# Linear attention on one core: half of one head's output stored by GpSimd's DMAs

## The chip, the cores and the metric

The kernel runs on one core of a Trainium2 chip. The metric is the time of one execution in device microseconds; the median of the three runs of the kernel before is 168.19 us (167.89 to 168.42). The core's engines are named as in the profile: PE (matrix multiplication; PEld is its weight load), DVE (vector), ACT (activation), POOL (GpSimd) and SP (which here only issues DMAs). Data moves between memory (HBM) and the core's own memory (SBUF) by 16 DMA engines that all issuers share.

## The reference

The input holds 32 heads of 2048 rows by 128 columns, in bfloat16. Each head is linear attention with the feature map elu + 1:

```
phi_q = where(q > 0, q + 1, exp(q)) + 1e-6
phi_k = where(k > 0, k + 1, exp(k)) + 1e-6
kv  = einsum("bhsd,bhse->bhde", phi_k, v)
z   = einsum("bhsd->bhd", phi_k)
num = einsum("bhqd,bhde->bhqe", phi_q, kv)
den = einsum("bhqd,bhd->bhq", phi_q, z)[..., None] + 1e-6
out = num / den
```

## The kernel before

**Layout.** A head lies in SBUF as 128 partitions ("rows" below) of 16 consecutive sequence rows, 16 x 128 bfloat16 values, 4 KB a partition and 512 KB a head. Partition p of the output tile is 4 KB of consecutive memory in the output.

**Stages of one head h.** SP loads k, v and q (`ldk`, `ldv`, `ldq`, line 388; for most heads two at once, 1 MB). phi is split in two parts: min(exp(x), 1) plus eps, and max(x, 0). For k, ACT computes the exponential (`ek`, L416), DVE clamps it (`em`, L392), and POOL makes the positive part (`rk`, L399). POOL also copies v beside a column of ones (`v1`, L429), so that one product gives kv and z. PE multiplies both parts into one accumulator (`kv`, L437) and DVE copies it out (`kvs`, L403). PE transposes q (`T`, L455); ACT and DVE make the two parts from it (`eq` L467, `emq` L392, `rqa` L397, `rqb` L398). PE multiplies with kv in two groups of tiles (`n`, L498, L503, L505), DVE takes the reciprocal of the denominator (`a` L522, `r` L525) and multiplies (`f`, L529) into one of 14 output buffers, `o_sb[:, h % 14]`. SP stores it (`st`, L538).

**Order.** Each engine runs a list of keys written out by hand in `ORDER`; `resolve` puts in the waits that the dependencies need and no others. An engine runs its list in order, so an operation that waits holds up all behind it on that engine. SP's list mixes loads and stores: with 14 output buffers the stores may come long after the computation, and many are put off to the end, where there is nothing left to load. `TIE` makes the positive part `rk` of head h wait for the clamp `em` of head h - 1, which places it behind DVE's clamps.

**Stores.** `st_parts(h)` gives the pieces of a head's store as (first tile, last tile, first row, last row). Most heads are one piece of all 128 rows. Head 2 is stored in pieces of 51, 64 and 13 rows, the first half of head 3 in pieces of 68 and 60, and head 31, the last, in three pieces by tiles as they become ready. Head 11, the twelfth, is one store, `st11.0`, placed behind the load of v for heads 28 and 29 and issued at 116.31 us. Its buffer is used again by head 25, whose multiplication `f25` waits for all stores of head 11.

**The end.** After its last store SP waits for each output buffer's semaphore in turn (L556), the last head's at the end.

POOL's list around the change is `... v121.0 v122.0 rk22.0 rk23.0 v123.0 rk24.0 v124.0 ...`. In the key `v122.0` the head is 22 and the last digit its piece: `v1` is the operation.

Of the kernel before, what the change touches and what calls it, by code (L numbers as in the profile page):

```python
# [14 lines left out]
NO, NE, NR, NV, NQ, NK = 14, 2, 2, 2, 4, 2  # L15
# [45 lines left out]
def groups(h):  # L61
    if h == NH - 1:
        return ((0, 2, 3, 0), (6, 2, 3, 2), (12, 2, 2, 4))
    return ((0, 4, 3, 0), (12, 2, 2, 4))
# [3 lines left out]
ROWS = {2: ((0, 51), (51, 115), (115, 128))}  # L68


def st_parts(h):
    tiles = ((0, 6), (6, 12), (12, 16)) if h == NH - 1 else WHOLE
    if h in HALF:
        tiles = HALVES
    return tuple((a, b, x, y) for i, (a, b) in enumerate(tiles)
                 for x, y in (HALF.get(h, ()) if i == 0 and h in HALF else ROWS.get(h, ((0, P),))))
# [5 lines left out]
def eps_dve(h, i):  # L82
    return i == 1 or h in EPD


def on(key, eng):
    return ON.get(key, eng)
# [11 lines left out]
def rqb_parts(h):  # L99
# [4 lines left out]
    if h == NH - 1:  # L104
# [48 lines left out]
    "POOL": """  # L153
        ident0 ident v10.0 v13.0 rk5.0 rk4.0 v14.0 v15.0 v16.0 rk6.0 rk7.0 v17.0 rk8.0 v18.0 v19.0 rk9.0
        rk10.0 v110.0 v111.0 rk11.0 v112.0 rk12.0 v113.0 rk13.0 v114.0 rk14.0 v115.0 rk15.0 v116.0 rk16.0
        rk17.0 v117.0 rk18.0 v118.0 v119.0 rk19.0 v120.0 rk20.0 rk21.0 v121.0 v122.0 rk22.0 rk23.0 v123.0
        rk24.0 v124.0 v125.0 rk25.0 v126.0 rk26.0 rk27.0 v127.0 v128.0 rk28.0 rk29.0 v129.0 rk30.0 v130.0
        rk31.0 v131.0
    """,
# [18 lines left out]
def _ap(base: bass.AP, elem_offset: int, dims):  # L178
    return bass.AP(base.tensor, base.offset + elem_offset, [list(base.ap[0])] + [list(d) for d in dims])


class Program:
# [10 lines left out]
    def add(self, eng, key, fn, deps=(), dma=None, inc=True):  # L193
        assert key not in self.op, key
        self.op[key] = (eng, fn, tuple(deps), dma, inc)
# [71 lines left out]
def bass_standalone__linear_attn_elu__prompt_kernel(nc: bass.Bass, q: bass.AP, k: bass.AP, v: bass.AP, out: bass.AP):  # L267
    B, H, S, D = q.shape
    assert D == P and S == 16 * P and B * H == NH
    NT = S // P  # L270
# [5 lines left out]
    qf, kf, vf, of = (t.rearrange("b h s d -> (b h) s d") for t in (q, k, v, out))  # L276
    rows = lambda t, h: t[h].rearrange("(p j) d -> p j d", j=NT)

    with ExitStack() as es:
        names = [0]  # L280

        def alloc(make, shape, dt):
            names[0] += 1
            return es.enter_context(make(f"la_{names[0]}", shape, dt))
# [5 lines left out]
        sb = lambda shape, dt=bf16: alloc(nc.sbuf_tensor, shape, dt)  # L290
# [6 lines left out]
        o_sb = sb([P, NO, NT, D])  # L297
# [7 lines left out]
        pr = Program(sem)  # L305
        add = pr.add
# [3 lines left out]
        def over(name, h, parts, t0, t1):  # L310
            return [f"{name}{h}.{i}" for i, (a, b) in enumerate(parts(h)) if a < t1 and t0 < b]

        def every(name, h, parts):
            return [f"{name}{h}.{i}" for i in range(len(parts(h)))]
# [8 lines left out]
        def used(buf, n, heads, key):  # L323
            for h in heads:
                u = users[buf, h % n]
                assert u[0] == h, (buf, h, u[0])
                u[2].append(key)

        def fs(h, banks):
            return [f"f{h}.{i}" for i, (t0, nb, n, b0) in enumerate(groups(h))  # L330
                    if set(banks) & set(range(b0, b0 + nb))]

        def both(h, p=pair):
            return (h - h % 2, h - h % 2 + 1) if p(h) else (h,)

        def first(h):
            return both(h)[0]

        def spans(h, t0, t1):
            if len(both(h)) == 1:  # L340
                return [(h, t0, t1)]
            at = [(x, *(min(max(t - 8 * (x - first(h)), 0), 8) * 2 for t in (t0, t1))) for x in both(h)]
            return [(x, a, b) for x, a, b in at if a < b]

        def rqs(h, t0=0, t1=NT):
            return [d for x, a, b in spans(h, t0, t1) for d in
                    ([f"rqa{x}"] if a < na(x) else []) + over("rqb", x, rqb_parts, a, b)]
# [57 lines left out]
        def head(h):  # L405
# [71 lines left out]
            if blk == len(two) - 1:  # L477
                for x in two:
                    out_of(x)

        def out_of(h):
            two, h0 = both(h), first(h)
            blk = h - h0

            def tile(buf, t):
                if len(two) == 1:
                    return buf[:, h % NQ, t]
                at = t % 8 * 2
                return buf[:, (h0 + t // 8) % NQ, at:at + 2].rearrange("p u d -> p (u d)").rearrange("p (m x) -> p m x", x=2)[:, :, blk]

            for i, (t0, nb, m, b0) in enumerate(groups(h)):
                late = eps_dve(h, i)

                def g(e, t0=t0, nb=nb, m=m, b0=b0, late=late):
                    for b in range(nb):
                        o = 512 * (b0 + b)
                        if not late:
                            e.matmul(_ap(o_ps[:, :], o + D, [[NC, m]]), lhsT=ones[:], rhs=epsr[:, 0:m], start=True,  # L498
                                     stop=False, skip_group_check=True)
                        for c in range(m):  # L500
                            t = t0 + b * m + c
                            to = o_ps[:, o + NC * c:o + NC * (c + 1)]
                            e.matmul(to, lhsT=tile(emq_sb, t), rhs=kvs_sb[:, h % NK, 0:NC], start=late and c == 0,  # L503
                                     stop=False, skip_group_check=True)
                            ins = e.matmul(to, lhsT=tile(rq_sb, t), rhs=kvs_sb[:, h % NK, 0:NC], start=False, stop=True,  # L505
                                           skip_group_check=True)
                    return ins
                banks = range(b0, b0 + nb)
                t1 = t0 + nb * m
                key = f"n{h}.{i}"  # L510
                add("PE", key, g, [d for x, a, b in spans(h, t0, t1) for d in over("emq", x, q_parts, a, b)] + [f"kvs{h}", "ones", "eps1", "eps2"] + rqs(h, t0, t1)
                    + (fs(h - 1, banks) if h else []) + ([f"kvs{h + 1}"] if 5 in banks and h + 1 < NH else []))
                for buf, n in (("emq", NQ), ("rq", NQ)):
                    used(buf, n, two, key)
                used("kvs", NK, (h,), key)
                den = _ap(o_ps[:, :], 512 * b0 + D, [[512, nb], [NC, m]])
                rden = rden_sb[:, h % 2, t0:t1].rearrange("p (a b) -> p a b", b=m)
                done = [key]
                if 5 in banks and h + 2 < NH and GAP == 3:
                    done += every("kv", h + 2, kv_parts) if on(f"kvs{h + 2}", "DVE") == "DVE" else [f"kvs{h + 2}"]  # L520
                if late:
                    add("DVE", f"a{h}.{i}", lambda e, rden=rden, den=den: e.tensor_scalar(  # L522
                        rden, den, EPS, None, op0=ALU.add), done)
                    done, den = [f"a{h}.{i}"], rden
                add("DVE", f"r{h}.{i}", lambda e, rden=rden, den=den: e.reciprocal(rden, den), done)  # L525

                def g(e, t0=t0, t1=t1, nb=nb, m=m, b0=b0):
                    first = lambda t: t.offset
                    return e.tensor_tensor(  # L529
                        out=_ap(o_sb[:, :, :, :], first(o_sb[:, h % NO, t0, 0:1]) - first(o_sb[:, :, :, :]),  # L530
                                [[m * D, nb], [D, m], [1, D]]),
                        in0=_ap(o_ps[:, :], 512 * b0, [[512, nb], [NC, m], [1, D]]),
                        in1=_ap(rden_sb[:, :, :], first(rden_sb[:, h % 2, t0:t0 + 1]) - first(rden_sb[:, :, :]),
                                [[m, nb], [1, m], [0, D]]), op=ALU.mult)
                add("DVE", f"f{h}.{i}", g, [f"r{h}.{i}"] + fill("o", NO, (h,), f"f{h}.{i}"))
            for i, (a, b, x, y) in enumerate(st_parts(h)):
                key = f"st{h}.{i}"
                add("SP", key, lambda e, a=a, b=b, x=x, y=y: e.dma_start(rows(of, h)[x:y, a:b], o_sb[x:y, h % NO, a:b]),  # L538
                    [f"f{h}.{j}" for j, (t0, nb, m, b0) in enumerate(groups(h)) if t0 < b and a < t0 + nb * m],
                    dma=f"o{h % NO}")  # L540
                used("o", NO, (h,), key)

        for h in range(NH):
            head(h)
# [7 lines left out]
        for e, engine in (("POOL", nc.gpsimd), ("SP", nc.sync), ("ACT", nc.scalar), ("PE", nc.tensor), ("DVE", nc.vector)):  # L552
            pr.emit(e, engine)
        last = f"o{(NH - 1) % NO}"
        for name in [f"o{s}" for s in range(NO) if f"o{s}" in pr.count and f"o{s}" != last] + [last]:
            nc.sync.wait_ge(pr.get(name), pr.count[name])  # L556


# [26 lines left out]
```

## Time and profile before

| what | value |
|---|---|
| median of the runs shown | 168.19 us |
| the profiled execution's own time | 167.83 us |
| its span, first to last instruction | 166.5 us |
| busy: PE, DVE, ACT, POOL | 156.6, 154.6, 146.6, 83.7 us |
| granted TensorE clock, mean | 0.994 |
| bytes read and written in HBM | 50.33 and 16.78 MB, 403 GB/s over the span |
| DMA packets | 16542 |
| head 11's output computed to its store's issue | about 77 to 116.31 us |
| store: issue to landing, median over the kernel | 15.5 us |

Times in the views are microseconds from the start of the span. A line such as `L399 POOL TENSOR_SCALAR` is a group of instructions by source line, engine and operation; the number in brackets behind a line of the timeline is the time the engine was idle before it and the one that ended that idle time. The DMA share is the mean over the 16 DMA engines. It can stand a little above 1, because packets of one engine overlap by a few per cent. The trace also records each arrival of a DMA at its semaphore. A DMA arrives once for each DMA engine that carries a share of it, so the spread of one DMA's 16 arrivals tells how far the 16 engines are apart.

### The profile page before, as it was taken

The page shows a single profiled execution, that of the slowest core. Times are in us where ns is not written, and L with a number is a line of the kernel's source. Part 1 is how long each engine was busy: PE and PEld are TensorE (multiplying, and loading weights), DVE is VectorE, ACT ScalarE, POOL GpSimd, SP SyncE. Part 2 cuts the span into 40 slices and gives each one's busy share as a digit, 9 for nine tenths or more (in the row PEclk, how much of TensorE's full clock was granted, in tenths as well). Part 3 has the DMA queues.
Part 4 walks back from the last instruction along what each step waited for, and adds up shares of the span by engine and source line. Part 5 has one row for each costly group of instructions (what it writes and reads, how often), then busy time and mean ns, then how long its engine had stood idle before and what let it go on. Part 6 is the DMA issues. An engine that isn't in the chain of part 4 may idle for free.

```text
span 166.5 us, 6111 instructions
## 1 busy us (share of the span) xinstructions
PE 156.6 (94%) x2709; PEld 150.9 (91%) x2709; DVE 154.6 (93%) x307; ACT 146.6 (88%) x99; POOL 83.7 (50%) x64
## 2 busy tenths in 40 slices
PE   4999997999999999999999999999999999999950
PEld 1677996999999999999999999999999999999840
DVE  0498999999999999999999999999999999999992
ACT  3799987899999999999999999999999999977700
POOL 1100019655666665555566666655655676634000
PEclk9999999999999999999999999999999999999997
DMA  5999999999999999999999999999999999999997
GB/s 224 410 424 411 422 403 418 403 405 404 420 418 412 414 406 427 411 423 410 417 408 423 415 424 404 420 415 424 407 416 422 413 416 414 416 416 413 385 396 279
DMA packets 16542, 67.51 MB, mean 405 GB/s; under 512 B 1539, under 2 KB 1923, under 8 KB 14723
## 3 DMA queue, kind: packets, MB, share of 16 engines
q1 hardware_dynamic: 16371, 66.59, 98.5%
q8 instruction: 21, 0.34, 0.8%
q10 hardware_dynamic: 144, 0.52, 0.8%
q14 instruction: 6, 0.05, 0.1%
HBM read 50.33 MB, written 16.78 MB: 403 GB/s over the span
## 4 chain that ended last, share of the span: by engine, by line
PE 83%; DMA 7%; DVE 6%; SPq 2%; issue 0%
PE la L437 33%; PE la L503 18%; PE la L505 16%; PE la L455 16%; DMA la<-in_q_dram 7%; DVE la L529 4%; SPq L388 2%; DVE la L398 1%; DVE la L525 1%; PE la L498 0%; DVE la L522 0%; DVE la L403 0%
## 5 line engine op out<-in xcount | busy, mean ns | idle before, releaser
L529 DVE TENSOR_TENSOR la<-la 128x1536 bf16<-128x1536 f32 (+1 forms) x65 | 77.9, 1200 | 0.6
L503 PE MATMUL la<-la 128*128 128x129 bf16 x512 | 66.6, 219 | 0.1
L505 PE MATMUL la<-la 128*128 128x129 bf16 x512 | 66.6, 219 | 0.0
L399 POOL TENSOR_SCALAR la<-la 128x2048 bf16<-128x2048 bf16 x28 | 53.0, 1893 | 26.2 <-DVE la L522 18.7
L467 ACT ACTIVATE la<-la 128x2048 bf16<-128x2048 bf16 (+2 forms) x35 | 60.2, 1728 | 5.0 <-PE la L455 3.1
L416 ACT ACTIVATE la<-la 128x2048 bf16<-128x2048 bf16 (+1 forms) x33 | 61.3, 1865 | 3.4 <-DMA la<-in_k_dram 1.9
L437 PE MATMUL la<-la 128*128 128x129 bf16 x1024 | 63.4, 220 | 0.0
L437 PEld LDWEIGHTS la<-la 128*128 128x128 bf16 x1024 | 59.3, 98 | 0.8 <-DVE la L403 0.4
L429 POOL COPY la<-la 128x1024 int32<-128x1024 int32 (+1 forms) x30 | 31.2, 1043 | 41.1 <-PE la L437 22.7
L505 PEld LDWEIGHTS la<-la 128*128 128x128 bf16 x512 | 49.8, 97 | 0.0
L503 PEld LDWEIGHTS la<-la 128*128 128x128 bf16 x512 | 48.1, 97 | 0.3 <-DVE la L529 0.2
L392 DVE TENSOR_SCALAR la<-la 128x2048 bf16<-128x2048 bf16 (+2 forms) x68 | 42.4, 658 | 1.1 <-ACT la L416 1.1
L455 PE MATMUL la<-la 128*128 128x128 bf16 x512 | 35.3, 222 | 1.0 <-DMA la<-in_q_dram 0.9
L455 PEld LDWEIGHTS la<-la 128*128 128x128 bf16 x512 | 30.7, 99 | 2.7 <-DMA la<-in_q_dram 1.5
L397 ACT ACTIVATE la<-la 128x1024 bf16<-128x1024 bf16 (+2 forms) x29 | 31.6, 1091 | 0.0
L398 DVE TENSOR_SCALAR la<-la 128x1024 bf16<-128x1024 bf16 (+2 forms) x36 | 24.4, 682 | 4.7 <-DMA la<-in_k_dram 4.6
L498 PE MATMUL la<-la 128*128 128x3 bf16 (+1 forms) x128 | 21.6, 168 | 2.5 <-DVE la L529 2.5
L498 PEld LDWEIGHTS la<-la 128*128 128x128 bf16 x128 | 12.5, 98 | 2.8 <-DVE la L529 2.8
L525 DVE RECIPROCAL la<-la 128x12 f32<-128x12 f32 (+1 forms) x65 | 12.9, 200 | 1.0 <-PE la L505 0.2
L403 DVE CAST la<-la 128x129 bf16<-128x129 f32 x32 | 8.3, 258 | 0.0
L368 PE MATMUL la<-la 128*128 128x480 bf16 x21 | 6.7, 468 | 1.5 <-POOL la L353 1.5
L368 PEld LDWEIGHTS la<-la 128*128 128x128 bf16 x21 | 2.3, 120 | 3.9 <-issue 1.7
(15 smaller groups left out, 9.7 us busy)
## 6 DMA issues: line engine op xcount, KB each, us to landing
out_dram<-la SPq DMA_DIRECT2D x29, 512.0 KB, 15.5
la<-in_q_dram SPq DMA_DIRECT2D x14, 1024.0 KB, 17.6
la<-in_v_dram SPq DMA_DIRECT2D x11, 1024.0 KB, 15.0
la<-in_k_dram SPq DMA_DIRECT2D x11, 1024.0 KB, 16.4
la<-in_k_dram SPq DMA_DIRECT2D x10, 512.0 KB, 13.5
la<-in_v_dram SPq DMA_DIRECT2D x9, 512.0 KB, 14.8
la<-in_q_dram SPq DMA_DIRECT2D x4, 512.0 KB, 10.3
la<-in_v_dram ACTq DMA_DIRECT2D x1, 512.0 KB, 5.6
```

What stands on the lines that cost most here:

```text
L392: add(on(key, "DVE"), key, lambda e: e.tensor_scalar(t, t, 1.0, EPS, op0=ALU.min, op1=ALU.add), deps)
L397: "ACT": lambda e: e.activation(dst, src, ACT.Relu),
L399: "POOL": lambda e: e.tensor_scalar(dst, src, BIG, 0.0, op0=ALU.min, op1=ALU.max)}[eng], deps)
L416: add("ACT", key, lambda e, a=a, b=b: e.activation(em_sb[:, h % NE, a:b], k_sb[:, h % NI["k"], a:b], ACT.Exp), [f"ldk{k0}.0"] + fill("em", ...
L429: add(on(key, "POOL"), key, lambda e, a=a, b=b, word=word: e.tensor_copy(v1_sb[:, h % NV, a:b, 0:D].bitcast(word), v_sb[:, h % NI["v"], a: ...
L437: ins = e.matmul(kv_ps, lhsT=src[:, j], rhs=v1_sb[:, h % NV, j, 0:NC], start=(j + part == 0), stop=(j == NT - 1 and part == 1))
L455: ins = e.transpose(to, src, ident[:])
L467: add("ACT", key, lambda e, a=a, b=b: e.activation(part(emq_sb, a, b), src(a, b), ACT.Exp), over("T", h, t_parts, a, b) + fill("emq", NQ, ...
L498: e.matmul(_ap(o_ps[:, :], o + D, [[NC, m]]), lhsT=ones[:], rhs=epsr[:, 0:m], start=True, stop=False, skip_group_check=True)
L503: e.matmul(to, lhsT=tile(emq_sb, t), rhs=kvs_sb[:, h % NK, 0:NC], start=late and c == 0, stop=False, skip_group_check=True)
L505: ins = e.matmul(to, lhsT=tile(rq_sb, t), rhs=kvs_sb[:, h % NK, 0:NC], start=False, stop=True, skip_group_check=True)
L529: return e.tensor_tensor(out=_ap(o_sb[:, :, :, :], first(o_sb[:, h % NO, t0, 0:1]) - first(o_sb[:, :, :, :]), [[m * D, nb], [D, m], [1, D] ...
```

## The change

Head 11's store by SP keeps rows 0 to 63, all 16 tiles. Rows 64 to 127 are stored by four DMAs that POOL issues: rows 64 to 73 (`swx`, 10 rows), 74 to 107 (`swa`, 34 rows), 108 to 110 (`swy`, 3 rows) and 111 to 127 (`swb`, 17 rows). Each of these DMAs names a row as two pieces of 2 KB, the second half first, on both sides, so the same bytes land in the same places. In POOL's list `swx` and `swa` stand behind `rk22.0`, `swy` and `swb` behind `v123.0`. Each waits for both groups of head 11's output, counts on a semaphore of its own, and is waited for by head 25's output and, first of all, at SP's end.

```
+SOFT = 11
+SPREAD = (("swx", 64, 74), ("swa", 74, 108), ("swy", 108, 111), ("swb", 111, 128))
+
+
 def st_parts(h):
+    if h == SOFT:
+        return ((0, 16, 0, 64),)
     tiles = ((0, 6), (6, 12), (12, 16)) if h == NH - 1 else WHOLE
...
     "POOL": """
-        rk17.0 v117.0 rk18.0 v118.0 v119.0 rk19.0 v120.0 rk20.0 rk21.0 v121.0 v122.0 rk22.0 rk23.0 v123.0
+        rk17.0 v117.0 rk18.0 v118.0 v119.0 rk19.0 v120.0 rk20.0 rk21.0 v121.0 v122.0 rk22.0 swx swa rk23.0 v123.0 swy swb
...
+            for key, x, y in SPREAD if h == SOFT else ():
+                half = NT * D // 2
+                sb, dr = o_sb[x:y, h % NO], rows(of, h)[x:y]
+                frm, to = (bass.AP(t.tensor, t.offset + half, [list(t.ap[0]), [-half, 2], [1, half]]) for t in (sb, dr))
+                add("POOL", key, lambda e, to=to, frm=frm: e.dma_start(to, frm),
+                    [f"f{h}.{j}" for j in range(len(groups(h)))], dma=key)
+                used("o", NO, (h,), key)
...
-        for name in [f"o{s}" for s in range(NO) if f"o{s}" in pr.count and f"o{s}" != last] + [last]:
+        for name in [x[0] for x in SPREAD] + [f"o{s}" for s in range(NO) if f"o{s}" in pr.count and f"o{s}" != last] + [last]:
             nc.sync.wait_ge(pr.get(name), pr.count[name])
```

## The prediction

> **What bounds the kernel now.** I read the page first (busy shares, the DMA row of the 40 slices, the queues), then the waits, the busy times in stretches of the tail, the store line L538, GpSimd's timeline around the new operations, and last the semaphore arrivals of each transfer that the trace records (one arrival for each DMA engine that takes part).
>
> The page, its second and third parts:
> ```profile
> DVE  0498999999999999999999999999999999999992
> DMA  5999999999999999999999999999999999999997
> ...
> q1 hardware_dynamic: 16371, 66.59, 98.5%
> ```
> DVE and the 16 DMA engines are both full almost to the end, so both are candidates. The busy times in stretches decide (DMA share is the mean over 16 engines):
> ```profile
> core 0: us, PE busy (x) PEld busy (x) DVE busy (x) ACT busy (x) POOL busy (x), PEclk, DMA share, GB/s
> ...
> 150.00:156.00 6.00, 6.00 (x112) 5.97 (x110) 5.66 (x11) 4.88 (x6) 1.85 (x2) 1.00 1.03 416
> 156.00:158.30 2.30, 1.98 (x34) 1.63 (x31) 2.23 (x8) 0.99 (x1) 0.00 (x0) 1.00 0.88 353
> 158.30:162.00 3.70, 2.09 (x36) 1.92 (x36) 3.60 (x10) 0.00 (x0) 0.00 (x0) 1.00 0.99 396
> 162.00:164.00 2.00, 0.00 (x0) 0.00 (x0) 1.38 (x2) 0.00 (x0) 0.00 (x0) 1.00 0.96 385
> 164.00:166.50 2.50, 0.00 (x0) 0.00 (x0) 0.00 (x0) 0.00 (x0) 0.00 (x0) 0.64 0.57 213
> ```
> After 164 no engine computes; only DMA runs, for 2.5 us, and with 0.57 of its engines. From 156.0 to 158.3 some already run dry (0.88). So the engines do not finish together. The waits of SP's own sequencer, and the store line from 155 on, agree:
> ```profile
> SPq L556 <- DMA out_dram<-la: 2.4, 2, 1.2
> ```
> ```profile
> L538 SPq DMA_DIRECT2D out_dram<-la x6: 332/333/537, 157.4 to 163.4; - x6
> ...
> DMA to landing us min/median/max: 5.3/5.7/6.1
> ```
> The arrivals give the skew. Head 28's store (512 KB, 8 rows of 4 KB per engine) reached its 16 counts at 156.64 us, then 0.07, 0.13, 3.12, 3.14, 3.24, 3.33, 3.91, 4.58, 4.58, 4.64, 4.70, 4.74, 4.75, 4.75 and 4.78 us later. **Three engines lead by 3.1 us, the last trails by 4.8.** From 130 us on every transfer has the 3.1 us step and ends 4.7 to 4.9 us after its first arrival, so the trailing engines never idle. At the end they go back to back: head 30's store ends at 165.18, then head 31's three stores need per engine 8 rows of 1536 B (64.9 ns), 1024 B (45.8) and 1536 B, together 1.40 us, so 166.58 against the 166.48 recorded. Without a backlog the last store could land at 165.23: issued 163.40, plus 1.31 us (head 31's first store, issued 161.63, first arrival 163.46, less 8 x 64.9 ns), plus 0.52. **The end is set by the most loaded DMA engines, 1.25 us after what the compute would allow.**
>
> **What goes.** SP's store of head 11 keeps rows 0 to 63. It gives each engine 8 rows now (128 rows over 16 arrivals); the half kept gives 4. So 4 rows of 4 KB leave every engine: 4 x 161.4 ns (mean packet of that size) = 0.65 us. One SP issue stays, its wait is the same.
>
> **What comes: where the 64 rows land.** The arrivals of before show how rows are shared: SP's store of 51 rows has 3 arrivals from engines, that of 68 has 4, of 60 has 15, of 13 has 13, of 64 or 128 has 16: always the largest number up to 16 that divides the rows. The three engines of the 51-row store took 17 rows each: right after it three stand 2.7 us further back (17 x 161.4 ns = 2.74). By that count 10, 34, 3 and 17 rows make 10, 2, 3 and 1 shares, of 1, 17, 1 and 17 rows: 16 shares in all. I take them to lie side by side on 16 different engines. Then 13 engines get one row (two 2 KB packets of 85.9 ns, 0.17 us), a net 0.65 - 0.17 = 0.47 us less; three get 17 rows, 17 x 0.172 - 0.65 = +2.28 us. If those three are the leaders (lead on the last 4.78), they still end 4.78 - 2.28 - 0.47 = 2.0 us ahead. No row shows where GpSimd's shares go; this is a choice, and the first rival is the other case. What the arrivals do show: if SP always deals from the first engine on, one leader is among the last three engines (it moves 0.12 us ahead just when SP's 13-row store passes three engines by), and none is among the first four (set back by the 51- and the 68-row store).
> The Trainium skill, DMA: Bandwidth & Descriptors, section "Why a DMA increments its semaphore by 16 and not by 1", states the same divisor rule, and that GpSimd's shares go on from a cursor that walks round the engines; started at 0, it would put the 17-row shares on engines 10, 11 and 15. That agrees with what the arrivals show of one leader; no run here shows the cursor.
>
> Small terms: arrivals cost a 4-byte packet of 9.1 ns; if each of the four DMAs posts on every engine, 0.04 us. So -0.47 + 0.04 = **-0.43 us** on the 13 engines. Bounds: -0.48 (3 rows by 161.4, no extras) and 0 (if reading the rows' descriptors costs as much as is saved; nothing in the trace shows that). I take -0.43, since it is the sum of measured packets. It arrives whole at the end, because those engines never idle after 116 us, where head 11 is stored.
>
> **What comes on GpSimd.** Two DMA issues stand after rk22 and two after v123. GpSimd's timeline, with those places (rk22 is the second line, rk23 and v123 the next two):
> ```profile
> 105.99 1.04 POOL L429 COPY la<-la 128x1024 int32<-128x1024 int32 x1 [1.61 <-PE la L437]
> 107.00 1.89 POOL L399 TENSOR_SCALAR la<-la 128x2048 bf16<-128x2048 bf16 x1
> 110.75 1.89 POOL L399 TENSOR_SCALAR la<-la 128x2048 bf16<-128x2048 bf16 x1 [1.85 <-DVE la L522]
> 112.58 1.04 POOL L429 COPY la<-la 128x1024 int32<-128x1024 int32 x1
> 115.37 1.89 POOL L399 TENSOR_SCALAR la<-la 128x2048 bf16<-128x2048 bf16 x1 [1.75 <-DVE la L522]
> ```
> Both places are idle gaps, 1.85 and 1.75 us. They wait only for head 11's output, which is some 40 us old. The trace has no issue by GpSimd. Low end: SP's, 0.33 us (L538). High end: GpSimd's longest usual operation, 1.89 us. I take 1.0, nearest to its copy (1.04), the one that only moves data. Two issues, 2.0 us, overrun each gap by some 0.2 us; at 1.89 by 2.0 us. Behind them queue rk23, v123 and rk24, v124, for which PE waits: rk23 and v123 end at 113.62 and their matmuls (L437) start at 117.81, 4.2 us of cover, and 4.62 us later again. Even the high end is covered on PE's side; SP's loads that wait for these reads are issued over 10 us ahead of landing.
>
> Not covered by that is DVE, which has no idle time here:
> ```profile
> 109.38 1.28 DVE L392 TENSOR_SCALAR la<-la 128x2048 bf16<-128x2048 bf16 x2
> ...
> 114.00 1.29 DVE L392 TENSOR_SCALAR la<-la 128x2048 bf16<-128x2048 bf16 x2
> ```
> GpSimd now idles just while these pairs run. Where the two meet early in a GpSimd operation, GpSimd gives way:
> ```profile
> 144.94 1.53 POOL L429 COPY la<-la 128x1024 int32<-128x1024 int32 x1
> ...
> 144.95 0.63 DVE L392 TENSOR_SCALAR la<-la 128x2048 bf16<-128x2048 bf16 x1
> ```
> The copy went from 1.04 to 1.53 us, DVE's operation stayed at 0.63. So I cost DVE at 0, with a bound of 1.9 us for each gap (a whole GpSimd operation ahead of DVE). A DVE delay d moves the last store's issue and the floor 165.23; the new end is 166.05, so the first 0.8 us cost nothing.
>
> Other edits: SP's four new waits at the end (28 ns each, steps of 0.07 us) fall between 163.74 and 165.2, while SP waits for DMA anyway: 0. Head 25's output overwrites the buffer: head 11's last arrival is now 134.04 against head 25's first multiplication at 135.62 (L529); SP's half comes 0.4 us earlier, and GpSimd's part is issued 20 us before: 0.
>
> **Sum.** The profiled execution took 167.83 us (span 166.5). 167.83 - 0.43 = 167.40. The median of the runs shown, 168.19, lies 0.36 above; so 168.19 - 0.43 = 167.76, forecast **167.75**, own range 167.6 to 168.1.
>
> **Rivals.**
> 1. *The shares fall elsewhere* (slower). Always from the first engine, as SP's do: it would carry 1 + 17 + 1 + 17 = 36 rows, 36 x 0.172 - 0.65 = +5.5 us, 173.7. A 17-row share on an engine that trails: +2.28, 170.5; on one that is 1.5 us ahead of the last: +0.8. It costs as soon as the share's 2.28 us exceed that engine's lead. For it: no row shows GpSimd's order. Against: one leader's place fits. 0.10.
> 2. *All four are dealt over 16 engines* in ceilings (1, 3, 1 and 2 rows each): the first three engines get 7 rows, 7 x 0.172 - 0.65 = +0.56, and they are among the last: 168.75, slower. For it: 128 and 64 rows are dealt so by SP; against: SP's 13, 51 and 60 rows are not. 0.06. The page named above states that GpSimd does deal some plain copies so.
> 3. *Issuing collides with DVE* (slower). If DVE is held up longer than 0.8 us, the floor decides: 1.5 us give 166.73 in the span, 168.4 against the median; 2 us give 168.9. For it: DVE saturated, the gaps coincide with its pairs; against: the overlap at 144.94. 0.16. The Trainium skill, SBUF — State Buffer, section "SBUF: two separate sides", warns that GpSimd cannot write descriptors while certain DVE copies run; by that, issues stall for at most 1.29 us a gap, covered as above, and the time stays the forecast's.
> 4. *Nothing moves*: the gain is spent on fetching descriptors or 2 KB packets under load: 168.0 to 168.4. 0.06.
>
> **Chances.** Forecast 0.62. About 0.3% (0.5 us) is what a measurement here can tell from no change; the forecast's 0.43 lies just inside, with the runs shown spread over 0.5 us, so I split it 0.36 faster, 0.26 within. Rival 3 gives 0.03 within, 0.13 slower; rival 4 0.01 faster, 0.05 within; 1 and 2 0.16 slower. Faster 0.37, within 0.34, slower 0.29. The range runs from 167.4 (0.48 and the runs' spread) to 168.9, which takes in rivals 2 and 4 and most of 3; rival 1 stays out.
>
> **What would show it.** Right: the arrivals' 3.1 us step falls to under 1 us, the 156 to 158.3 stretch has a share near 1.0, the last arrival comes about 0.4 us earlier, packets of 2 KB rise by 128. Wrong: one arrival of late transfers 2 us or more behind all others (rival 1); DVE idle before L392 or longer L392 around 109 to 119 and the last L529 later (rival 3).

## The result, and the profile after

The changed kernel takes **170.12 us** (median of 4 runs, 169.79 to 171.03) against 168.12 for the kernel before on the same chip: ratio 1.0127 [1.0082, 1.0172]. It is slower by 2.0 us, where 167.75 and a range of 167.4 to 168.9 were forecast. The profiled execution is the longest of the four, 171.03 us with a span of 169.7. Lines of kernel.py from 72 on stand lower in the changed file: the store by SP is now L544, SP's waits at the end L569, DVE's clamp L398, GpSimd's positive part L405 and its copy L435; GpSimd's DMAs are issued at L552.

The page of the kernel after, its slices and its queues:
```profile
DVE  0499899999999999999999999999999999999970
DMA  5999999999999999999999999999999999999982
...
q1 hardware_dynamic: 16307, 66.33, 96.4%
...
q0 software_dynamic: 640, 0.27, 0.6%
```
DVE is done a slice earlier than the span, and the last DMA slice holds a 2: few DMA engines work there. The new queue q0 is GpSimd's. It moved 0.27 MB, which is the 64 rows, but in 640 packets.

The busy times in stretches of the tail after (columns as before):
```profile
core 0: us, PE busy (x) PEld busy (x) DVE busy (x) ACT busy (x) POOL busy (x), PEclk, DMA share, GB/s
156.00:158.30 2.30, 2.30 (x45) 2.24 (x42) 2.27 (x9) 2.05 (x2) 0.00 (x0) 1.00 0.91 370
158.30:162.00 3.70, 2.21 (x39) 1.92 (x37) 3.52 (x8) 0.00 (x0) 0.00 (x0) 1.00 0.95 375
162.00:164.00 2.00, 0.62 (x13) 0.45 (x9) 2.00 (x6) 0.00 (x0) 0.00 (x0) 1.00 0.96 387
164.00:166.50 2.50, 0.00 (x0) 0.00 (x0) 0.43 (x1) 0.00 (x0) 0.00 (x0) 1.00 0.64 243
166.50:169.70 3.20, 0.00 (x0) 0.00 (x0) 0.00 (x0) 0.00 (x0) 0.00 (x0) 0.59 0.11 42
```
The last 3.2 us have no engine at work and a DMA share of 0.11, and 0.11 x 16 is about 1.8 engines. The wait at SP's end (total, times, longest) says the same:
```profile
SPq L569 <- DMA out_dram<-la: 4.3, 2, 3.3
```
The store line from 155 us on shows where the extra time sits: the stores are issued 1.1 us later than before and then take 7.3 to 8.2 us to land instead of 5.3 to 6.1.
```profile
L544 SPq DMA_DIRECT2D out_dram<-la x6: 332/333/434, 158.4 to 164.5; - x6
...
DMA to landing us min/median/max: 7.3/7.8/8.2
```
Who is late, the 16 arrivals of head 28's store tell (us after the first, from the trace):
```
before 0.00 0.07 0.13 3.12 3.14 3.24 3.33 3.91 4.58 4.58 4.64 4.70 4.74 4.75 4.75 4.78
after  0.00 0.13 2.30 3.04 3.13 3.14 3.17 3.32 3.82 4.39 4.46 4.56 4.59 4.84 7.83 7.99
```
Of the three leaders **one** fell back by about 2.2 us, to 2.30. Two are still in front. And two arrivals that have no match before stand at 7.83 and 7.99: these are two engines that did not lead and were given 17 rows. They carry the excess to the end. Not all of it is the length of the shares: in the load of v landing from 128.6 us on the two stood at 5.57 and 5.62, in the store after it at 6.38 and 6.51, where the trace has two packets of over 1 us at 134.2 us (last section). Later each fell back by another 1.5 us, much as five engines do in the kernel before, which go from at most 3.4 to 4.6 and more between head 11's store and head 28's. The last store is issued at 164.46; by the way of the prediction the compute would allow an end at 164.46 + 1.31 + 0.52 = 166.29, and the last arrival comes at 169.61.

The second surprise is on GpSimd and DVE. GpSimd's timeline after:
```profile
109.13 1.72 POOL L552 DMA_DIRECT2D out_dram<-la  x2
111.47 1.88 POOL L405 TENSOR_SCALAR la<-la 128x2048 bf16<-128x2048 bf16 x1 [0.63 <-DVE la L528]
...
114.30 1.59 POOL L552 DMA_DIRECT2D out_dram<-la  x2
116.52 1.88 POOL L405 TENSOR_SCALAR la<-la 128x2048 bf16<-128x2048 bf16 x1 [0.62 <-DVE la L528]
```
DVE's timeline after, the clamp pairs at the same places:
```profile
109.67 1.70 DVE L398 TENSOR_SCALAR la<-la 128x2048 bf16<-128x2048 bf16 x2
114.68 1.74 DVE L398 TENSOR_SCALAR la<-la 128x2048 bf16<-128x2048 bf16 x2
```
The four issues take 0.73, 0.98, 0.62 and 0.98 us (0.83 in the mean; 1.0 was taken) and fit the gaps: GpSimd idles 0.6 us behind each pair. But each clamp pair lasts 1.70 and 1.74 us instead of 1.28 and 1.29. The starts of the heads' first multiplications (1536 elements, L535) show what that does: against before they lie 0.3 us later from head 2 on, which no part of the change can cause, 0.68 later at head 20, 1.11 at head 21, and then stay at 1.1. So DVE lost 0.8 us beside the issues, where 0 was taken.

### The profile page after: what moved, and what is told of

It reads as the page before. It is cut to its first block, busy times and chain, and to the rows that moved or that the text cites. A ratio compares the mean times of both kernels' runs of the same rounds, so it can differ in the third digit from the quotient of the medians.

```text
span 169.7 us, 6119 instructions
## 1 busy us (share of the span) xinstructions
PE 157.4 (93%) x2709; PEld 151.7 (89%) x2709; DVE 155.5 (92%) x307; ACT 146.7 (86%) x99; POOL 87.7 (52%) x68
## 4 chain that ended last, share of the span: by engine, by line
DVE 57%; PE 37%; DMA 2%; issue 1%
DVE la L535 29%; PE la L443 14%; DVE la L398 14%; DVE la L404 7%; PE la L461 7%; PE la L509 6%; PE la L511 6%; DVE la L531 4%; PE la L374 3%; DVE la L409 2%; DMA la<-in_q_dram 2%; DVE la L528 1%; PE la L504 0%
## 5 line engine op out<-in xcount | busy, mean ns | idle before, releaser
L535 DVE TENSOR_TENSOR la<-la 128x1536 bf16<-128x1536 f32 (+1 forms) x65 | 77.9, 1199 | 0.6
L405 POOL TENSOR_SCALAR la<-la 128x2048 bf16<-128x2048 bf16 x28 | 53.0, 1895 | 24.0 <-DVE la L528 16.3
L435 POOL COPY la<-la 128x1024 int32<-128x1024 int32 (+1 forms) x30 | 31.9, 1064 | 40.6 <-PE la L443 22.3
L398 DVE TENSOR_SCALAR la<-la 128x2048 bf16<-128x2048 bf16 (+2 forms) x68 | 42.9, 665 | 1.1 <-ACT la L422 1.1
L374 PE MATMUL la<-la 128*128 128x480 bf16 x21 | 7.3, 502 | 1.5 <-POOL la L359 1.5
```

What stands on the lines that cost most here:

```text
L398: add(on(key, "DVE"), key, lambda e: e.tensor_scalar(t, t, 1.0, EPS, op0=ALU.min, op1=ALU.add), deps)
L405: "POOL": lambda e: e.tensor_scalar(dst, src, BIG, 0.0, op0=ALU.min, op1=ALU.max)}[eng], deps)
L435: add(on(key, "POOL"), key, lambda e, a=a, b=b, word=word: e.tensor_copy(v1_sb[:, h % NV, a:b, 0:D].bitcast(word), v_sb[:, h % NI["v"], a: ...
L535: return e.tensor_tensor(out=_ap(o_sb[:, :, :, :], first(o_sb[:, h % NO, t0, 0:1]) - first(o_sb[:, :, :, :]), [[m * D, nb], [D, m], [1, D] ...
```

## The experiments

The ideas to be told apart: **place** (a share of 17 rows costs time where it falls on an engine that does not lead), against **count** (four more DMAs, or DMAs by GpSimd at all), **issue** (GpSimd's issuing holds up DVE and so the end), **form** (the reversed halves by themselves) and **size** (a share of 17 rows costs by itself). Below, "place 0 to 15" counts the shares of GpSimd's DMAs in the order of issue. In the change, places 0 to 9 take one row each, 10 and 11 take 17, 12 to 14 one, and 15 takes 17. Every kernel stores the whole output. The first four ran on one chip (before 168.12 there, 25 runs), the next four on another (168.15, 25 runs), the last two on a third (168.23, 11 runs). Edits are shown against the changed kernel.

**even4**: the same four places in GpSimd's list, four shares of 16 rows, so that no engine gets more than one row of a DMA.
```
-SPREAD = (("swx", 64, 74), ("swa", 74, 108), ("swy", 108, 111), ("swb", 111, 128))
+SPREAD = (("swx", 64, 80), ("swa", 80, 96), ("swy", 96, 112), ("swb", 112, 128))
```


> Rows 64 to 127 in four GpSimd DMAs of 16 rows each, at the same places; every DMA engine gets 4 rows, as SP's store would give it. Theory A (the time comes from 17-row shares on two DMA engines that were not ahead): the late step behind the main group goes, the time is 168.1 to 168.7 us, although the two DVE clamps are still stretched by about 0.4 us each and the last store is issued about 1 us later. Theory B (the time comes from GpSimd's issues holding up DVE): the time stays near 170.

Measured: 168.13 us, ratio 0.9999 [0.9987, 1.0012]. GpSimd's and then DVE's timeline of even4:
```profile
109.86 1.33 POOL L552 DMA_DIRECT2D out_dram<-la  x2
...
114.62 1.20 POOL L552 DMA_DIRECT2D out_dram<-la  x2
```
```profile
110.41 1.29 DVE L398 TENSOR_SCALAR la<-la 128x2048 bf16<-128x2048 bf16 x2
115.03 1.28 DVE L398 TENSOR_SCALAR la<-la 128x2048 bf16<-128x2048 bf16 x2
```
Issues are shorter (0.56 to 0.68 us), the clamps keep their 1.28 us, and the leaders still stand 3.1 us ahead. So four DMAs by GpSimd with reversed halves cost nothing: count and form fall as causes of the loss. The issue does not fall yet, since no clamp is stretched here.

**one64**: one DMA of 64 rows, four on each engine.
```
-SPREAD = (("swx", 64, 74), ("swa", 74, 108), ("swy", 108, 111), ("swb", 111, 128))
+SPREAD = (("swx", 64, 128),)
...
-        ... v122.0 rk22.0 swx swa rk23.0 v123.0 swy swb
+        ... v122.0 rk22.0 swx rk23.0 v123.0
```


> Rows 64 to 127 in a single GpSimd DMA of 64 rows behind rk22. Theory A: 168.0 to 168.5. Theory B: one clamp stretched instead of two, about half of the 2 us, so near 169. The 8-byte packets on GpSimd's queue: if each DMA costs each engine 8 of them, 128 in all; if they go with rows or bytes, 512 again.

Measured: 168.13 us, ratio 1.0013 [0.9992, 1.0034]. Whether SP or GpSimd carries the rows makes no difference.

**lead15**: only the last share of 17 rows, at place 15, with 15 single rows before it; SP keeps rows 0 to 95.
```
-SPREAD = (("swx", 64, 74), ("swa", 74, 108), ("swy", 108, 111), ("swb", 111, 128))
+SPREAD = (("swx", 96, 111), ("swb", 111, 128))
...
-        return ((0, 16, 0, 64),)
+        return ((0, 16, 0, 96),)
...
-        ... v122.0 rk22.0 swx swa rk23.0 v123.0 swy swb
+        ... v122.0 rk22.0 swx rk23.0 v123.0 swb
```


> Only rows 96 to 127 by GpSimd: 15 rows (15 shares of one), then 17 rows (one share); SP stores rows 0 to 95. Theory A with the shares walking on from the first engine: the 17-row share falls on the engine that was a leader in the arrivals, it drops from 0.1 to about 2.4 us behind the first, nobody falls behind the main group's 4.8, time 167.9 to 168.5. If the walk starts elsewhere, another engine moves 2.4 us back. Theory B: about 169 to 170, since both gaps still hold an issue.

Measured: 168.19 us, ratio 1.0000 [0.9986, 1.0014]. Head 28's arrivals begin 0, 0.22, 2.32 and end at 4.83: one leader takes the 17 rows, nobody falls behind the others, and no time is lost. Place 15 is a leader.

GpSimd's issue of that share in lead15, and DVE's clamps there:
```profile
114.95 1.02 POOL L552 DMA_DIRECT2D out_dram<-la  x1
```
```profile
110.73 1.29 DVE L398 TENSOR_SCALAR la<-la 128x2048 bf16<-128x2048 bf16 x2
115.36 1.70 DVE L398 TENSOR_SCALAR la<-la 128x2048 bf16<-128x2048 bf16 x2
```
The 15-row issue (0.74 us) leaves the pair beside it at 1.29 us, the 17-row issue (1.02) stretches its pair to 1.70.

**find**: to find the two other leaders, heads 11, 12 and 14 each get a pair of 17-row shares, at places 4 and 5, 6 and 7, 8 and 9. SP stores rows 0 to 63 and 112 to 127 of these heads, and the lists of SP and GpSimd name the new DMAs.
```
+SPREAD = {11: (("swx", 64, 68), ("swa", 68, 102), ("swy", 102, 112)),
+          12: (("sxx", 64, 70), ("sxa", 70, 104), ("sxy", 104, 112)),
+          14: (("szx", 64, 72), ("sza", 72, 106), ("szy", 106, 112))}
...
+    if h in SPREAD:
+        return ((0, 16, 0, 64), (0, 16, 112, 128))
```


> A search for the other two leading DMA engines, no candidate for speed: heads 11, 12 and 14 each store rows 64 to 111 by GpSimd (4, 34 and 10 rows; 6, 34 and 8; 8, 34 and 6), SP the rest. If the shares walk on from the first engine, the pairs of 17-row shares fall on engines 4 and 5, then 6 and 7, then 8 and 9, one pair after another. Theory A: where a pair meets a leader, a leading arrival drops back by about 2.2 us; where it does not, two arrivals of the main group fall back by as much and the time rises with them, to 170 or more. Theory B predicts nothing of the arrivals and about 172 (three times the issues).

Measured: 170.17 us (one run). After head 11's pair no leader had moved and two of the main group fell back; after head 12's one leader dropped to 2.4; after head 14's another. One leader is thus at 6 or 7, one at 8 or 9. Places 10 and 11 hold none.

**pair78**: the change with 7, 34, 6 and 17 rows, so that the 17-row shares sit at places 7, 8 and 15.
```
-SPREAD = (("swx", 64, 74), ("swa", 74, 108), ("swy", 108, 111), ("swb", 111, 128))
+SPREAD = (("swx", 64, 71), ("swa", 71, 105), ("swy", 105, 111), ("swb", 111, 128))
```


> As the changed kernel, but with 7, 34, 6 and 17 rows, so that by the walk the 17-row shares fall on engines 7, 8 and 15. Theory A (only the place of the shares decides): the search put one leader among 6 and 7 and one among 8 and 9. If 7 and 8 are the leaders, all three leading arrivals drop by about 2.3 us, the largest lag stays near 4.8 and the time is 167.7 to 168.2; with one of them wrong, one arrival lies 2 to 3 us behind the main group and the time is 169 to 170. Theory C (any 17-row share slows the kernel, through the queue's packets or stalls, wherever it lies): near 170.

Measured: **168.21 us**, ratio 1.0000 [0.9985, 1.0015]. The loss is gone, although the issues take as long as in the changed kernel (0.62 to 0.98 us) and both clamp pairs are stretched (1.70 and 1.73 us): the issue falls as its cause. Two stretches of pair78's tail (columns as above):
```profile
156.00:158.30 2.30, 2.30 (x46) 2.30 (x44) 2.27 (x9) 2.22 (x2) 0.00 (x0) 1.00 1.03 420
...
164.00:166.50 2.50, 0.00 (x0) 0.00 (x0) 0.61 (x1) 0.00 (x0) 0.00 (x0) 1.00 0.73 275
```
All engines are now busy from 156 to 158.3 (1.03, where before showed 0.88), and the spread of head 28's arrivals falls from 4.78 to 2.52 us. That is the picture the prediction described for the change. Yet the time is that of before, for two reasons. The engines that were to be relieved gain nothing that can be told: the last arrivals lie 0.22 us behind those of the same transfers before in the ten that land from 93 to 111.6 us, ahead of GpSimd's rows, and 0.26 to 0.41 us behind from 134 us on (one trace each). And the stretched clamps, with 0.45 us of a later start, put the last store's issue at 164.63. It could land at 166.46, and it lands at 166.84, so little was left to win.

**pair10**: the change without its last 17-row share: 10, 34 and 4 rows, and SP stores rows 112 to 127 (`st11.1` in its list, behind `st11.0`).
```
-SPREAD = (("swx", 64, 74), ("swa", 74, 108), ("swy", 108, 111), ("swb", 111, 128))
+SPREAD = (("swx", 64, 74), ("swa", 74, 108), ("swy", 108, 112))
...
-        return ((0, 16, 0, 64),)
+        return ((0, 16, 0, 64), (0, 16, 112, 128))
```


> Of the changed kernel's DMAs only 10, 34 and 4 rows, so only the pair of 17-row shares; SP stores rows 0 to 63 and 112 to 127. Theory A: the two misplaced shares alone make the loss: the two late arrivals stay, all three leaders stay in front, time 169.3 to 170.5. Theory C: two thirds of the loss, about 169.4, if each share costs the same.

Measured: 170.50 us (4 runs, 170.40 to 170.52), ratio 1.0125 [1.0097, 1.0153]. Its wait at the end:
```profile
SPq L569 <- DMA out_dram<-la: 3.2, 2, 2.1
```
Its last stretch:
```profile
166.50:169.70 3.20, 0.00 (x0) 0.00 (x0) 0.00 (x0) 0.00 (x0) 0.00 (x0) 0.58 0.11 41
```
All three leaders stay in front (0, 0.02, 0.15), two arrivals stand at 7.12 and 7.28, and the same 0.11 closes the span. The pair at 10 and 11 alone makes the whole loss.

**heavy6_9**: six DMAs of 6, 17, 2, 17, 5 and 17 rows, which put the 17-row shares at places 6, 9 and 15, to settle which of each pair leads.
```
-SPREAD = (("swx", 64, 74), ("swa", 74, 108), ("swy", 108, 111), ("swb", 111, 128))
+SPREAD = (("swx", 64, 70), ("swa", 70, 87), ("sws", 87, 89), ("swt", 89, 106), ("swy", 106, 111), ("swb", 111, 128))
...
-        ... rk22.0 swx swa rk23.0 v123.0 swy swb
+        ... rk22.0 swx swa sws rk23.0 v123.0 swt swy swb
```


> The 17-row shares one by one on engines 6, 9 and 15 (6, 17, 2, 17, 5 and 17 rows). Theory A: the complement of the run with 7 and 8: each leader that was missed there is hit here; with both missed here, two arrivals lie about 2.3 us or more behind the main group and the time is near 170. Theory C: near 170 in both.

Measured: 170.03 us, ratio 1.0086 [1.0055, 1.0118]. Two leaders stay (0, 0.01), two arrivals stand behind the rest at 5.16 and 5.34: 6 and 9 do not lead, so 7 and 8 do. The ten runs fall in two groups, 168.62 to 168.98 (four) and 169.93 to 170.61 (six). The profiled run is of the lower one. In it the late pair stands only 0.6 us behind the last arrival of before (4.78). The last store is issued at 165.43, since the run starts 1.05 us late and the clamps are stretched, and the last arrival comes 1.97 us later with a spread of 0.19 us: there the compute sets the end. The upper group may be one more packet of instruction code (16 KB, 1.0 us) on a late engine, but no trace of an upper run was taken, so this is argued only.

**plain**: each row named as one run of 4 KB in place of two reversed halves.
```
-                frm, to = (bass.AP(t.tensor, t.offset + half, [list(t.ap[0]), [-half, 2], [1, half]]) for t in (sb, dr))
+                frm, to = sb, dr
```


> The changed kernel with each row as one run of 4 KB instead of its second and then its first half. If the form of the rows decides how they are dealt, the 34 and 17 rows are dealt over all 16 engines in ceilings of 3 and 2: no share of 17 rows, no arrival 2 us behind, the first three engines 3 rows more, time 168.0 to 168.8. If it doesn't, the arrivals and the time stay as with the changed kernel, near 170.

Measured: 168.61 us, ratio 1.0023 [1.0008, 1.0038]. No share of 17 rows is left. The arrivals begin 0, 0.82, 1.47 and end at 5.53: the rows are dealt in ceilings, and the first engines get most, as the second rival described (168.75 by its sum). The reversed halves are what makes large shares. No clamp is stretched (1.28 and 1.29 us).

**tied78**: pair78 with the 34- and the 17-row DMA waiting for DVE's clamps `em22` and `em23`, so that they are issued after the clamps and not beside them.
```
+BEHIND = {"swa": ["em22.0"], "swb": ["em23.0"]}
...
-                    [f"f{h}.{j}" for j in range(len(groups(h)))], dma=key)
+                    [f"f{h}.{j}" for j in range(len(groups(h)))] + BEHIND.get(key, []), dma=key)
```


> As the run with the shares on engines 7, 8 and 15, but the 34-row and the 17-row DMA wait for DVE's clamp of head 22 or 23, so that they are issued behind DVE's pair of clamps and not while it runs. If only an issue under way holds a clamp up, both clamps go back to 1.29 us a pair, the multiplications of heads 20 and 21 lose their 0.4 us steps and the last store is issued 0.8 us earlier; the time stays at 168.0 to 168.2, because the end is set by the DMA engines, which win only 0.1 us. If the delay moves on (GpSimd's copy now reaches into the next pair), a step of 0.4 us or more comes back one head later.

Measured: 169.30 us, ratio 1.0070 [1.0051, 1.0090]; slower than pair78. GpSimd's timeline (L406, L436 and L553 here):
```profile
111.33 0.98 POOL L553 DMA_DIRECT2D out_dram<-la  x1 [1.40 <-DVE la L532]
112.34 1.91 POOL L406 TENSOR_SCALAR la<-la 128x2048 bf16<-128x2048 bf16 x1
114.18 1.04 POOL L436 COPY la<-la 128x1024 int32<-128x1024 int32 x1
...
119.55 1.04 POOL L436 COPY la<-la 128x1024 int32<-128x1024 int32 x1
120.78 1.27 POOL L436 COPY la<-la 128x1024 int32<-128x1024 int32 x1 [0.19 <-PE la L444]
```
DVE's clamps (L399 here):
```profile
109.73 1.28 DVE L399 TENSOR_SCALAR la<-la 128x2048 bf16<-128x2048 bf16 x2
114.35 2.04 DVE L399 TENSOR_SCALAR la<-la 128x2048 bf16<-128x2048 bf16 x2
119.77 2.82 DVE L399 TENSOR_SCALAR la<-la 128x2048 bf16<-128x2048 bf16 x2
```
The pair that was to be spared keeps its 1.28 us. But GpSimd is now late, and its copies start 0.17 and 0.22 us before the next pairs, which grow to 2.04 and 2.82 us; beside the second pair a second copy runs. Head 21 is 0.74 us later, head 22 another 1.54. The last store goes out at 165.98 and the last arrival is at 167.94, 1.96 later, with a spread of the arrivals of 0.22 us: here the compute sets the end. The wait at SP's end is down to the store's own landing:
```profile
SPq L570 <- DMA out_dram<-la: 1.1, 1, 1.1
```

**heavy31**: the same with 32 rows by SP and 7, 29, 23, 6 and 31 by GpSimd, the large shares at 7, 8 and 15. In GpSimd's list `sws` stands behind `v123.0`, `swy` and `swb` behind `v125.0`.
```
+SPREAD = (("swx", 32, 39), ("swa", 39, 68), ("sws", 68, 91), ("swy", 91, 97), ("swb", 97, 128))
+BEHIND = {"swa": ["em22.0"], "sws": ["em23.0"], "swb": ["em24.0"]}
...
+        return ((0, 16, 0, 32),)
```


> Shares as far as the leaders bear: SP stores rows 0 to 31, GpSimd 7, 29, 23, 6 and 31 rows, the three large ones on engines 7, 8 and 15 and tied behind the clamps. By packets a light engine carries 3 rows instead of 8, 5 x 0.161 = 0.81 us less, and at most 40 packets of 8 bytes and 5 arrivals more, 45 x 0.009 = 0.41: 0.4 us net. The leader with 31 rows goes 25 x 0.16 + 0.4 = 4.4 us back, as far as the last now lies. Theory A: time 167.6 to 168.0, if DVE is not held up more than 0.5 us; 168.0 to 168.5 if it is. Theory C (large shares cost something in themselves): over 169.

Measured: 169.66 us, ratio 1.0093 [1.0073, 1.0113]. Shares of 23 to 31 rows on the leaders push no engine behind: head 28's arrivals spread over 2.33 us and 15 of them over 1.68. Size by itself falls: the time is no lower because DVE lost 2.6 us at heads 21 to 23, and the last store's issue, 166.39, sets the end.

No version was faster than the kernel before; pair78, even4, one64 and lead15 equal it.

## Why the prediction was wrong, point by point

- **What bounds the kernel: right.** The skew of the DMA engines sets the end in the kernels before, after and pair10. It stops doing so where the last store goes out late enough (tied78, heavy31, the profiled run of heavy6_9).
- **"I take them to lie side by side on 16 different engines": right.** The size of a 17-row share, 2.28 us, was about right too. With 0.43 us less on the other leaders, the one at place 15 was to fall 2.7 us back against them; it fell back by about 2.2 in the kernel after and in lead15. So the 2.28 us fit, and the 0.43 us do not (below).
- **"If those three are the leaders": the step that failed.** The arrivals of before supported one leader among the last three engines and excluded the first four. For the other two they said nothing, and the text let all three be leaders. They are at places 7, 8 and 15 (lead15, find, pair78, heavy6_9); the change loads 10, 11 and 15. With the pair on 7 and 8 the loss is gone, with the pair on 10 and 11 alone it is complete. The first rival in its form "a 17-row share on an engine that trails: +2.28, 170.5" is what happened: 170.12 and, in pair10, 170.50. Its other form, "on one that is 1.5 us ahead of the last: +0.8", is closer to the late pair of heavy6_9, which ended 0.6 us behind the last of before. The rival had a chance of 0.10, although only one of the three places had any support in a row. In the Trainium skill's page DMA: Bandwidth & Descriptors, section "Why a DMA increments its semaphore by 16 and not by 1", the walk of GpSimd's shares over consecutive engines agrees with these runs, and its exception for some direct copies with the run plain; neither could tell which engines lead.
- **"-0.43 us on the 13 engines": mis-sized.** Beside the rows, q0 carries 512 packets of 8 bytes that no view of before showed, 9 ns each. Shared evenly (the trace does not name the engine of a packet) these are 32 an engine, 0.29 us, and 0.04 for the arrivals. Of the 0.48 us of three rows 0.15 would remain by this estimate. Measured: no gain that can be told in pair78, whose last arrivals lie 0.22 us behind those of before ahead of the change and 0.26 to 0.41 behind after it. The two halves of a row also travel as one packet of 4 KB (159 ns), not as two of 85.9.
- **The issues on GpSimd: right** in place and about right in size. rk23, v123 and rk24 stay covered.
- **"So I cost DVE at 0": wrong, but hidden in its effect.** The clamp pairs lost 0.42 and 0.45 us, inside the bound of 1.9. In the kernel after this is covered, since the end lies 3.3 us behind what the compute allows. In pair78 the cover is nearly gone, in tied78 (2.3 us lost) wholly. The one overlap in the trace of before, where GpSimd gave way, did not bear the rule taken from it: in tied78, where GpSimd's copy starts first, DVE waits. That agrees with the Trainium skill's page SBUF — State Buffer, section "SBUF: two separate sides", by which, of a GpSimd operation and a DVE operation of certain kinds, whichever starts first keeps the ports they share; no run here shows whether the clamps are of these kinds.
- **The waits at the end and head 25's reuse: right**, no view shows a cost.

## What to carry to other kernels

Before a transfer is made uneven to fill up engines that run ahead, it has to be measured which engines these are, and not only how many: runs with large shares at known places (lead15, find) showed it here. Shares that miss can cost most of their length (2.3 us in pair10, where 17 rows take 2.7), while shares that hit gain only what the other engines give up (nothing that could be told in pair78), so the odds of the place need to be far better than even. An average gain over 13 engines is also to be set against what the DMAs add by themselves: packets that are in no row of before, and a neighbour engine held up. And of the lead of 3.1 us no more than 1.25 us could be won, because there the floor set by the compute comes next.

## What the runs showed of the hardware

- **Small packets.** GpSimd's DMAs of reversed halves with 10, 34, 3 and 17 rows bring 512 packets of 8 bytes, those of 7, 34, 6 and 17 (pair78) 512, of 15 and 17 (lead15) 256, of 7, 29, 23, 6 and 31 (heavy31) 1264; those of 16 rows (even4) and of 64 (one64) none, nor has any in the form of plain. What they are stays open.
- **Arrivals of GpSimd's DMAs.** The kernel after has 64 packets of 4 bytes on q0 and 16 arrivals for each of its four GpSimd DMAs, also for the one of 17 rows, which is a single share; an SP store of 51 rows has 3 arrivals from engines. So one arrival for each engine with a share holds for SP's DMAs only.
- **Two queues on one engine.** The 4 KB packets of one 17-row share start 0.46 us apart while SP's 8 KB packets (0.31 us) run and 0.31 us apart later, beside SP's 4 KB packets, as if the two queues took turns. The 34 rows in the kernel after were served from 114.3 to 120.5 us, so 17 rows of 0.16 us, 2.7 us in all, took some 6 us.
- **Issue and clamp.** Issues of 0.55 to 0.76 us leave the clamps beside them as they are; those of a share of 17 rows (0.98 to 1.02 us) stretch them by 0.41 to 0.45 us a pair. Why that is so stays open.
- **Two long packets.** In the profiled run of the kernel after, two packets of 4 KB took 1.06 and 1.13 us at 134.2 us, where 0.16 is usual, and the two late arrivals rise by 0.8 and 0.9 us just there. This run is the longest of the four; whether the others have such packets is not known. pair10 has none and is as slow, so the loss does not hang on them. Where they come from stays open.
- **The start scatters.** The first heads' multiplications lie 0.2 to 1.4 us later than before in traces of other kernels, ahead of any edit. Where the DMA engines set the end, this hardly shows: even4 starts 1.03 us later and spans 166.7 us, against 166.5.
